# Turned queries first, weighted values last, and pooling kept to two steps of four, in a fused attention and feed-forward kernel

## The chip, the cores and the metric

The kernel runs on one core of one Trainium2 chip. The metric is device time in microseconds (us); less is better. Five engines work side by side, each through its own queue in order: TensorE (PE, matrix products), VectorE (DVE), ScalarE (ACT), GpSimd (POOL), and SyncE (SP), which here issues every DMA.

## What is computed

Attention over pooled keys and values, and a feed-forward layer with squared ReLU on its result, all in float32:

```python
# q, k, v: (8 batches, 8 heads, 576 tokens, 64)
k_p = k.reshape(B, H, Sp, 8, D).mean(axis=3)        # Sp = 72
v_p = v.reshape(B, H, Sp, 8, D).mean(axis=3)
scores = scale * np.matmul(q, k_p.transpose(0, 1, 3, 2))
attn = np.exp(scores - max); attn = attn / (sum + 1e-09)
x = np.matmul(attn, v_p) -> (4608 tokens, 512)
h = np.maximum(x @ w_in, 0.0)                        # w_in 512 x 2048
out = h * h @ w_out                                  # w_out 2048 x 512
```

The weights come in as float64 and are turned into float32 on the chip.

## The kernel before

The 4608 tokens are cut into 12 chunks (`c`) of 384. The 2048 hidden columns are cut into 16 pieces (`fc`) of 128. A *step* is one pair (c, fc); there are 192, and the loop at line 653 runs over them. In step s PE makes the hidden piece of that step (`hidden`, tile `h`, 12 products) and, two steps late (`LAG`), the product with `w_out` (`project`, tile `o`, 9 products; the first chunk has fewer). From the second chunk on, each factor is split into a high and a low part (`xh`, `xl`; `gh`, `gl`; weights `w_i`, `w_o` in two halves), so that three cheap products replace a costly one. In between, ACT and DVE take the hidden piece through ReLU (ACT, tile `r`), square (DVE, `r`), cast (ACT, `gh`) and difference (DVE, `gl`).

The attention of the chunks to come is worked in among these steps. Each chunk has four head pairs (`p`), and a pair goes through eight stages (line 637), whose steps `STEADY` sets for chunks 2 to 11 (line 80; chunk 1 has `EARLY`, chunk 0 stands ahead of the loop): `transpose_q` at step 16c - 22 + 4p, then `scores`, `exponents`, `send_sums`, `fetch_sums`, `reciprocals`, `fetch_reciprocals` and `weigh_values` 1, 3, 4, 5, 6, 7 and 8 steps later. So the steps repeat in fours. Counted by the step number modulo 4:

- 2: `transpose_q` of one pair (PE `qps`; ACT casts its high part into `st`, DVE writes the difference into `st`) and `weigh_values` of another (PE `av`; DVE multiplies into `rb`, ACT casts `xh`, DVE writes `xl`). I call this the turn step.
- 3: `scores` (PE `sps`, which reads all of `st`; ACT copies to `sc`; POOL reduces the maximum over partitions, `mx`).
- 0: `reciprocals` (DVE `rr`, from the DMA `rc`).
- 1: `exponents` (DVE and ACT on `sc`; POOL sums over partitions, `tot`).

Keys and values of a batch must be pooled before its first chunk. `kv_steps` (line 625) sets this with `KV0`, the step of its start, and `KV_AT`, four lists of offsets: key loads and reductions (`load_k`, `pool_k`, DVE `kp`), the turns of the two halves of the keys (`transpose_k`, PE `kps`), and value loads; a value is reduced (`pool_v`, DVE `vp`) two steps after its load. All loads of `q`, `k` and `v` share four buffers (`LD`, tag `ld`), and a load waits in SP's queue until its buffer is free. Six batches go this way; the first two are pooled ahead of the steps.

The order within a step is written out in the loop: `hidden`; the PE work of the step's other items, in the order of the list `later`; `project`; the split of the hidden piece of the step before; then what each item of `later` returned (its ACT and DVE work), in the same order; then the items without PE work, pooling among them; the conversion and the splitting of weights; the loads; and last the ReLU. Every engine keeps this order. Three PSUM buffers (`ps_a`) serve `qps`, `kps`, `av` and `sps` in turn.

Of the kernel before, what the change touches and what calls it, by code (L numbers as in the profile page):

```python
# [32 lines left out]
def pooled_attn_relu2_ffn(  # L33
# [44 lines left out]


    STEADY = ((-22, -18, -14, -10), (0, 1, 3, 4, 5, 6, 7, 8))  # L80
    KV0 = -31
    EARLY = ((-19, -16, -13, -10), (0, 2, 3, 5, 5, 6, 7, 8))

    KV_AT = ((0, 1, 2, 3, 4, 5), (2, 3, 4, 5, 6, 7), (5, 8), (6, 7, 8, 9, 10, 11, 12, 13))
    NKT = H * SP_ // QT
    WC = 256

# [18 lines left out]
    def issue_loads():  # L106
        for dst, src in loads:
            dma(dst, src)
        loads.clear()
# [37 lines left out]
    def to_float32(*keys):  # L147
        parts = []
        for key in keys:
            words, m = raw.pop(key).rearrange("p a (n w) -> p a n w", w=2), wf[key].rearrange("p (a n) -> p a n", a=2)  # L150
            parts.append((words, m, m.bitcast(U32)))
        for _, m, _ in parts:
            DVE.tensor_scalar(m, m, EXP_MIN, EXP_MAX, op0=ALU.max, op1=ALU.min)
        for _, _, m in parts:
            DVE.tensor_scalar(m, m, 3, 0x3FFFFFF8, op0=ALU.logical_shift_left, op1=ALU.bitwise_and)
        for words, _, m in parts:
            DVE.scalar_tensor_tensor(m, words[..., 1], 0xC0000000, m, op0=ALU.bitwise_and, op1=ALU.bitwise_or)
        for words, _, m in parts:
            DVE.scalar_tensor_tensor(m, words[..., 0], 29, m, op0=ALU.logical_shift_right, op1=ALU.bitwise_or)
# [320 lines left out]
    def hidden(c, fc):  # L480
        hp = ps_h.tile([P, 512], F32, name=f"h_{c}_{fc}", tag="h")
        cb, o = fc * P // WC, fc * P % WC
        prods = []
        for cc in range(NCC):
            key, cols = ("i", cb, cc // 2 * 2), slice(cc % 2 * WC + o, cc % 2 * WC + o + P)
            if c == 0:
                prods += [(wf[key][:, cols], xts[c][:, cc, :])]
            else:
                prods += [(wt[key][:, w, cols], xts[c][x][:, cc, :]) for w, x in ((0, 0), (0, 1), (1, 0))]
        for i, (w, x) in enumerate(prods):  # L490
            PE.matmul(hp[:, :CH], lhsT=w, rhs=x, start=i == 0, stop=i == len(prods) - 1)

        def activate():
            if c == 0:
                r = sb.tile([P, CH], F32, name=f"r_{c}_{fc}", tag="gh", bufs=LAG + 1)
            else:
                r = sb.tile([P, CH], F32, name=f"r_{c}_{fc}", tag="r", bufs=2)
            ACT.activation(r, hp[:, :CH], AF.Relu)
            if c < 2:
                ACT.activation(r, r, AF.Square)  # L500
            else:
                DVE.tensor_tensor(r, r, r, op=ALU.mult)
            gts[c, fc] = r

        return activate

    def split_hidden(c, fc):
        if c == 0:
            return
        gh = sb.tile([P, CH], F32R, name=f"gh_{c}_{fc}", tag="gh", bufs=LAG + 1)  # L510
        gl = sb.tile([P, CH], F32R, name=f"gl_{c}_{fc}", tag="gl", bufs=LAG + 1)
        split(gh, gl, gts[c, fc])
        gts[c, fc] = (gh, gl)
# [3 lines left out]
    def project(c, fc):  # L517
        if fc == 0:
            accs[c] = [ps_o.tile([P, 512], F32, name=f"o_{c}_{t}", tag=f"o{t}") for t in range(NTT)]
        g, key = gts.pop((c, fc)), ("o", fc)  # L520
        for t in range(NTT):
            tt = slice(t * P, (t + 1) * P)
            if c == 0:
                prods = [(g[:, tt], wf[key])]
            else:
                prods = [(g[x][:, tt], wt[key][:, w, :]) for x, w in ((0, 0), (0, 1), (1, 0))]
            for i, (a, w) in enumerate(prods):
                PE.matmul(accs[c][t], lhsT=a, rhs=w, start=fc == 0 and i == 0, stop=fc == NFC - 1 and i == len(prods) - 1)

        def store():  # L530
            for t in range(NTT):
                ob = sb.tile([P, DM], F32, name=f"ob_{c}_{t}", tag="ob", bufs=OB)
                ACT.copy(ob, accs[c][t])
                dma(out[c * CH + t * P:c * CH + (t + 1) * P, :], ob)

        return store if fc == NFC - 1 else None
# [88 lines left out]
    def kv_steps(b, s):  # L625
        k_at, pool_at, turn_at, v_at = KV_AT
        for i in range(NKT):
            at(s + k_at[i], load_k, b, i)
            at(s + pool_at[i], pool_k, b, i)
        for hf in range(2):  # L630
            at(s + turn_at[hf], transpose_k, b, hf)
        for h in range(H):
            at(s + v_at[h], load_v, b, h)
            at(s + v_at[h] + 2, pool_v, b, h)
# [3 lines left out]
    for c in range(1, NCH):  # L638
        first, offsets = EARLY if c == 1 else STEADY
        for b, _, _ in segments(c):  # L640
            if b not in ready:
                ready.add(b)
                kv_steps(b, c * NFC + KV0)
        for p in range(NPAIR):
# [7 lines left out]
    on_pe = (transpose_q, transpose_k, scores, token_scores, token_turn, weigh_values)  # L652
    for s in range(-PRO, len(steps) + LAG):
        todo = work.get(s, [])
        activate = hidden(*steps[s]) if 0 <= s < len(steps) else None
        later = [f(*a) for f, a in todo if f in on_pe]
        store = project(*steps[s - LAG]) if s >= LAG else None
        if 0 <= s - 1 < len(steps):
            split_hidden(*steps[s - 1])
        for f in later:  # L660
            f()
        for f, a in todo:
            if f not in on_pe + last:
                f(*a)
        keys = [a[0] for f, a in todo if f is to_float32]
        if keys:
            to_float32(*keys)
        for f, a in todo:
            if f is split_weights:
                f(*a)  # L670
        issue_loads()
        for f in (activate, store):
            if f:
                f()
# [30 lines left out]
```

## Time and profile before

| | us |
|---|---|
| median of the runs (985.11, 985.27, and one of 3297.35) | 985.27 |
| profiled execution | 978.9 |
| its span, from the first to the last instruction | 977.2 |
| PE busy | 947.3 (97%) |
| DVE busy | 629.2 (64%) |
| ACT busy | 425.8 (44%) |
| POOL busy | 401.2 (41%) |

Instructions of all helpers have one line in the trace (L29), so they are told apart by the tiles that they write and read: `st<-qps,st` is DVE's difference for turned queries, `sps<-st,kl` a product of the scores. A busy PE is not PE at its peak, since its matrix products overlap; how fast it goes is read from the starts of equal pieces of work. The granted clock is the share of TensorE's full 2.4 GHz.

### The profile page before, as it was taken

How to read it: one execution, taken by the hardware profiler on the slowest of the kernel's cores; microseconds unless marked ns; L12 is line 12 of the kernel's file. 1: busy time of each engine (PE TensorE's matmuls, PEld its weight loads, DVE VectorE, ACT ScalarE, POOL GpSimd, SP SyncE). 2: the span in 40 equal slices, each digit the busy share in tenths (PEclk: the TensorE clock that was granted, in tenths of full speed). 3: DMA queues.
4: the chain of work that ended last, by engine and by line, in shares of the span. 5: the costliest groups of instructions: out<-in, count | busy, mean ns of one | idle time of the engine just before them, and what ended most of it. 6: DMA issues, size and time to landing. Idle time of an engine off the chain costs nothing.

```text
span 977.2 us, 13363 instructions
## 1 busy us (share of the span) xinstructions
PE 947.3 (97%) x4888; PEld 785.9 (80%) x4888; DVE 629.2 (64%) x1034; ACT 425.8 (44%) x847; POOL 401.2 (41%) x209
## 2 busy tenths in 40 slices
PE   6889989999999999999999999999999999999998
PEld 5544458878888888888888888888888888888997
DVE  5869997886775555776776554777677455453221
ACT  2745457674334344334434434433443434432322
POOL 4398635463444434343435335343534434340000
PEclk9999999999999999999999999999999999999999
DMA  9944203112211002112112001211221100100000
GB/s 244 354 147 163 82 17 98 49 51 82 60 56 49 25 26 74 57 52 87 49 50 74 19 23 60 66 48 36 98 57 43 58 26 17 58 10 9 33 1 32
DMA packets 53361, 64.45 MB, mean 66 GB/s; under 512 B 14936, under 2 KB 34480, under 8 KB 53296
## 3 DMA queue, kind: packets, MB, share of 16 engines
q1 hardware_dynamic: 53296, 63.61, 20.9%
q8 instruction: 38, 0.62, 0.3%
q14 instruction: 27, 0.22, 0.1%
HBM read 53.87 MB, written 9.71 MB: 65 GB/s over the span
## 4 chain that ended last, share of the span: by engine, by line
PE 77%; DVE 13%; issue 5%; ACT 4%; POOL 0%; DMA 0%; POOLq 0%; DVEq 0%; ACTq 0%; SPq 0%
PE o L29 34%; PE h L29 33%; PE sps L29 3%; PE av L29 3%; DVE wf_o L29 3%; DVE wf_i L29 2%; PE qps L29 2%; DVE st L29 2%; DVE r L29 1%; ACT st L29 1%; DVE vp L29 1%; DVE sc L29 1%; ACT gh L29 1%; DVE rb L29 1%; ACT xh L29 1%
## 5 line engine op out<-in xcount | busy, mean ns | idle before, releaser
L29 PE MATMUL h<-xh,w_i 128*128 128x384 f32 x1408 | 389.0, 337 | 0.0
L29 PE MATMUL o<-w_o,gh 128*128 128x512 f32 x1056 | 333.7, 397 | 0.0
L29 POOL PARTITION_ALL_REDUCE tot<-sc x88 | 250.2, 2890 | 192.5 <-issue 179.3
L29 PEld LDWEIGHTS h<-xh,w_i 128*128 128x128 f32 x1408 | 258.7, 188 | 8.4 <-issue 0.5
L29 POOL PARTITION_ALL_REDUCE mx<-sc x88 | 138.2, 1618 | 268.8 <-ACT sc L29 268.8
L29 PE MATMUL h<-xl,w_i 128*128 128x384 f32 x704 | 237.9, 338 | 0.0
L29 PEld LDWEIGHTS o<-w_o,gh 128*128 128x128 f32 x1056 | 193.4, 189 | 32.8 <-issue 1.2
L29 DVE TENSOR_TENSOR gl<-r,gh 128x384 fp32r<-128x384 f32 x176 | 142.6, 810 | 107.8 <-ACT gh L29 107.0
L29 PE MATMUL o<-w_o,gl 128*128 128x512 f32 x528 | 209.0, 396 | 0.0
L29 DVE TENSOR_TENSOR r<-r 128x384 f32<-128x384 f32 x160 | 101.7, 635 | 113.7 <-ACT r L29 113.2
L29 ACT CAST gh<-r 128x384 fp32r<-128x384 f32 x176 | 90.4, 514 | 179.8 <-DVE r L29 179.3
L29 ACT ACTIVATE r<-h 128x384 f32<-128x384 f32 x192 | 94.0, 490 | 106.3 <-PE h L29 105.5
L29 PEld LDWEIGHTS h<-xl,w_i 128*128 128x128 f32 x704 | 132.1, 188 | 8.2 <-issue 0.7
L29 PEld LDWEIGHTS o<-w_o,gl 128*128 128x128 f32 x528 | 99.1, 188 | 22.2
L29 ACT CAST xh<-rb 128x384 fp32r<-128x384 f32 x44 | 22.6, 513 | 136.6 <-DVE rb L29 136.6
L29 DVE TENSOR_TENSOR st<-qps,st 64x384 fp32r<-64x384 f32 x80 | 60.6, 757 | 32.6 <-ACT st L29 32.1
L29 ACT ACTIVATE sc<-sc 72x384 f32<-72x384 f32 x88 | 43.7, 525 | 74.1 <-DVE sc L29 74.1
L29 ACT CAST st<-qps 64x384 fp32r<-64x384 f32 x80 | 59.0, 738 | 0.5
L29 DVE TENSOR_REDUCE vp<-v 72x64 f32<-72x512 f32 x48 | 51.0, 1064 | 0.4
L29 DVE TENSOR_REDUCE kp<-k 96x64 f32<-96x512 f32 x42 | 44.1, 1049 | 3.7 <-DMA k<-in_k_dram 3.7
L29 DVE TENSOR_TENSOR sc<-sc,mx 72x384 f32<-72x384 f32 x88 | 44.5, 545 | 0.0
L29 DVE TENSOR_TENSOR rb<-av,rb 128x384 f32<-128x384 f32 x44 | 24.4, 555 | 30.1 <-PE av L29 29.9
(82 smaller groups left out, 725.9 us busy)
## 6 DMA issues: line engine op xcount, KB each, us to landing
k<-in_k_dram SPq DMA_DIRECT2D x48, 192.0 KB
out_dram<-ob SPq DMA_DIRECT2D x36, 256.0 KB
rb<-rd SPq DMA_DIRECT2D x88, 96.0 KB
raw_i<-in_moe_w_in_dram SPq DMA_DIRECT2D x16, 512.0 KB
raw_o<-in_moe_w_out_dram SPq DMA_DIRECT2D x16, 512.0 KB
v<-in_v_dram SPq DMA_DIRECT2D x48, 144.0 KB
q<-in_q_dram SPq DMA_DIRECT2D x30, 192.0 KB
q<-in_q_dram SPq DMA_DIRECT2D x32, 96.0 KB
```

The costliest lines, as they stand in the source:

```text
L29: return lambda *a, **k: self.tc.keep_in_program_order(f(*a, **k))
```

## The change

Three numbers or tables and one line differ.

```diff
-    KV0 = -31
+    KV0 = -35
-    KV_AT = ((0, 1, 2, 3, 4, 5), (2, 3, 4, 5, 6, 7), (5, 8), (6, 7, 8, 9, 10, 11, 12, 13))
+    KV_AT = ((0, 1, 4, 5, 8, 9), (2, 3, 6, 7, 10, 11), (7, 12), (12, 13, 16, 17, 20, 21, 24, 25))
...
-        later = [f(*a) for f, a in todo if f in on_pe]
+        later = [f(*a) for f, a in sorted(((f, a) for f, a in todo if f in on_pe), key=lambda x: x[0] is weigh_values)]
```

`KV0` and all offsets of pooling now make its steps 3 or 0 modulo 4; the turns of keys fall into steps 0 and 1. A batch takes 28 steps from its first load to its last reduction, where it took 16; the first keys are loaded four steps earlier. The sort puts `weigh_values` behind all else in the list `later`, on PE and, since the list is also the order of what follows, on ACT and DVE.

On PE, in the turn step at chunk 4, piece 10 (`h_10`, then `av` of chunk 5 and `qps` of chunk 6), the kernel before has:

```order
 L29 MATMUL h_10_3917<-xh_2838,w_i_2_1574 128x384
 L29 MATMUL av_2_3930<-sc_2_3619,vp_2276 64x384 x2
 L29 MATMUL qps_0_3933<-ident,q_0_3776 128x96 x4
 L29 MATMUL o_0_3553<-w_o_1519,gh_8_3894 128x512 x2
 L29 MATMUL o_0_3553<-w_o_1519,gl_8_3895 128x512
```

and the changed kernel:

```order
 L29 MATMUL h_10_3912<-xh_2833,w_i_2_1573 128x384
 L29 MATMUL qps_0_3925<-ident,q_0_3776 128x96 x4
 L29 MATMUL av_2_3930<-sc_2_3628,vp_2185 64x384 x2
 L29 MATMUL o_0_3562<-w_o_1519,gh_8_3890 128x512 x2
 L29 MATMUL o_0_3562<-w_o_1519,gl_8_3891 128x512
```

`qps` and `av` have changed places; nothing else has.

On DVE, from the exponents of step 73 to the scores' step 75 (`r_9` to `gl_10`), the kernel before has:

```order
 L29 TENSOR_TENSOR sc_3_3814<-sc_3_3814,mx_3_1_3816 72x384
 L29 TENSOR_REDUCE vp_3741<-v_0_3825 72x64
 L29 TENSOR_TENSOR r_9_3914<-r_9_3914 128x384
 L29 TENSOR_TENSOR gl_9_3948<-r_9_3914,gh_9_3947 128x384
 L29 TENSOR_TENSOR rb_2_3900<-av_2_3930,rb_2_3900 128x384
 L29 TENSOR_TENSOR xl_3544<-rb_2_3900,xh_3543 128x384
 L29 TENSOR_TENSOR st_0_3954<-qps_0_3933,st_0_3954 64x2x2x96 x2
 L29 TENSOR_REDUCE vp_3741<-v_1_3863 72x64
 L29 TENSOR_TENSOR r_10_3967<-r_10_3967 128x384
 L29 TENSOR_TENSOR gl_10_3999<-r_10_3967,gh_10_3998 128x384
 L29 TENSOR_REDUCE vp_3741<-v_2_3912 72x64
```

and the changed kernel:

```order
 L29 TENSOR_TENSOR sc_3_3814<-sc_3_3814,mx_3_1_3815 72x384
 L29 TENSOR_TENSOR r_9_3909<-r_9_3909 128x384
 L29 TENSOR_TENSOR gl_9_3943<-r_9_3909,gh_9_3942 128x384
 L29 TENSOR_TENSOR st_0_3946<-qps_0_3925,st_0_3946 64x2x2x96 x2
 L29 TENSOR_TENSOR rb_2_3896<-av_2_3930,rb_2_3896 128x384
 L29 TENSOR_TENSOR xl_3558<-rb_2_3896,xh_3557 128x384
 L29 TENSOR_TENSOR r_10_3961<-r_10_3961 128x384
 L29 TENSOR_TENSOR gl_10_3993<-r_10_3961,gh_10_3992 128x384
 L29 TENSOR_REDUCE vp_3657<-v_0_3907 72x64
```

`st` stands ahead of `rb` and `xl`, and the two reductions before and behind them (`vp`) are gone; the first value of this batch is reduced behind `gl_10`.

Where two batches follow each other at once, their pooling overlaps now. DVE at chunk 2, pieces 2 to 4 (steps 35 and 36), before:

```order
 L29 TENSOR_TENSOR gl_2_2151<-r_2_2119,gh_2_2150 128x384
 L29 TENSOR_REDUCE kp_0_2163<-k_0_2051 96x64
 L29 COPY kp_0_2163<-kp_0_2163 96x64
 L29 TENSOR_TENSOR r_3_2168<-r_3_2168 128x384
 L29 TENSOR_TENSOR gl_3_2194<-r_3_2168,gh_3_2193 128x384
 L29 TENSOR_SCALAR rr_1_2197<-rc_1_2161 96x8
 L29 RECIPROCAL rr_1_2197<-rr_1_2197 96x8
 L29 TENSOR_REDUCE kp_0_2163<-k_1_2116 96x64
 L29 COPY kp_0_2163<-kp_0_2163 96x64
```

and now:

```order
 L29 TENSOR_TENSOR gl_2_2152<-r_2_2120,gh_2_2151 128x384
 L29 TENSOR_REDUCE vp_1384<-v_4_2037 72x64
 L29 TENSOR_REDUCE kp_0_1968<-k_2_2049 96x64
 L29 COPY kp_0_1968<-kp_0_1968 96x64
 L29 TENSOR_TENSOR r_3_2167<-r_3_2167 128x384
 L29 TENSOR_TENSOR gl_3_2200<-r_3_2167,gh_3_2199 128x384
 L29 TENSOR_TENSOR kl_2184<-kps_0_2186,kh_2183 128x288
 L29 TENSOR_REDUCE vp_1384<-v_5_2111 72x64
 L29 TENSOR_SCALAR rr_1_2206<-rc_1_2163 96x8
 L29 RECIPROCAL rr_1_2206<-rr_1_2206 96x8
 L29 TENSOR_REDUCE kp_3_2211<-k_3_2116 96x64
 L29 COPY kp_3_2211<-kp_3_2211 96x64
```

Each of these two steps has a value of one batch and a key of the next; before, each had a key alone, and the steps after them had one each too.

## Rows read from the trace of the kernel before

**Rows 1.** Stretch, length, busy us of PE, PEld, DVE, ACT, POOL; clock, DMA share, GB/s

```profile
30.00:150.00 120.00, 109.55 (x426) 58.51 (x424) 104.46 (x188) 64.77 (x129) 76.09 (x24) 0.99 0.43 140
...
210.00:540.00 330.00, 327.63 (x1727) 283.08 (x1726) 219.39 (x345) 141.66 (x285) 139.26 (x70) 1.00 0.18 56
```

**Rows 2.** Waits, whole span: engine, tile, awaited: total us, times, longest

```profile
DVE rr L29 <- DMA rc<-rs: 7.6, 1, 7.6
...
PE sps L29 <- DVE st L29: 8.5, 9, 2.3
```

**Rows 3.** Timeline of PE around `av`: start us, us, engine, line, what

```profile
152.04 0.87 PE L29 MATMUL av<-sc,vp 72*64 72x384 f32 x4
...
324.59 0.87 PE L29 MATMUL av<-sc,vp 72*64 72x192 f32 x8
...
343.13 0.34 PE L29 MATMUL h<-xh,w_i 128*128 128x384 f32 x1
343.39 0.87 PE L29 MATMUL av<-sc,vp 72*64 72x192 f32 x8
...
877.24 0.87 PE L29 MATMUL av<-sc,vp 72*64 72x384 f32 x4
```

**Rows 4.** Timeline of PE around one turn of keys

```profile
263.17 0.34 PE L29 MATMUL h<-xh,w_i 128*128 128x384 f32 x1
263.34 0.41 PE L29 MATMUL kps<-ident,kp 96*128 96x96 f32 x3
263.54 0.71 PE L29 MATMUL o<-w_o,gh 128*128 128x512 f32 x2
```

**Rows 5.** Timeline of all engines around one wait, steps 74 and 75; brackets: idle before

```profile
419.82 1.92 DVE L29 TENSOR_TENSOR gl<-r,gh 128x384 fp32r<-128x384 f32 x1 [0.58 <-ACT gh L29]
420.00 0.55 PE L29 MATMUL qps<-ident,q 96*128 96x96 f32 x4
...
422.24 0.51 ACT L29 CAST xh<-rb 128x384 fp32r<-128x384 f32 x1 [2.45 <-DVE rb L29]
422.66 1.70 ACT L29 CAST st<-qps 64x384 fp32r<-64x384 f32 x2
...
424.39 1.67 DVE L29 TENSOR_TENSOR st<-qps,st 64x384 fp32r<-64x384 f32 x2 [1.04 <-ACT st L29]
...
426.21 0.37 PE L29 MATMUL sps<-st,kl 128*72 128x384 f32 x1 [1.45 <-DVE st L29]
```

**Rows 6.** Timeline of DVE and PE at steps 14 and 15

```profile
130.99 0.54 DVE L29 TENSOR_TENSOR rb<-av,rb 128x384 f32<-128x384 f32 x1
...
133.71 1.70 DVE L29 TENSOR_TENSOR st<-qps,st 64x384 fp32r<-64x384 f32 x2 [1.04 <-ACT st L29]
...
135.55 0.46 PE L29 MATMUL sps<-st,kl 128*72 128x384 f32 x1 [2.29 <-DVE st L29]
...
137.70 1.92 DVE L29 TENSOR_TENSOR w_i<-wf_i,w_i 128x512 fp32r<-128x512 f32 x2
```

**Rows 7.** Timeline of DVE and POOL in the round after rows 5

```profile
426.10 1.06 DVE L29 TENSOR_REDUCE vp<-v 72x64 f32<-72x512 f32 x1
...
428.63 2.87 POOL L29 PARTITION_ALL_REDUCE mx<-sc  x2 [6.46 <-ACT sc L29]
...
429.67 0.55 DVE L29 TENSOR_TENSOR r<-r 128x384 f32<-128x384 f32 x1
...
443.81 1.68 DVE L29 TENSOR_TENSOR st<-qps,st 64x384 fp32r<-64x384 f32 x2 [1.04 <-ACT st L29]
```

**Rows 8.** Instructions of tiles `r` and `kp`: ns least/median/most, first and last start

```profile
L29 DVE TENSOR_TENSOR gl<-r,gh x176: 541/559/1991, 145.7 to 968.9; 128x384 fp32r<-128x384 f32 x176
...
L29 DVE TENSOR_REDUCE kp<-k x42: 998/1052/1094, 3.5 to 718.9; 96x64 f32<-96x512 f32 x42
L29 DVE COPY kp<-kp x42: 190/193/933, 4.5 to 719.9; 96x64 f32<-96x64 f32 x42
```

**Rows 9.** PE by stretch: busy, granted clock, DMA share, GB/s

```profile
136.00:138.00 2.00, 2.00 (x6) 0.50 0.03 8
```

## The prediction

> **What bounds the kernel now.** I read busy times by stretch first: in the long middle, 210 to 540 us, TensorE (PE) is busy 327.63 of 330 us, VectorE (DVE) 219.39 [rows 1]. So only two things count there: what PE executes, and where it stands still. The waits say where: of all that PE waits for, one line repeats, the scores `sps` waiting for DVE's `st`, 8.5 us in 9 waits, the longest 2.3 [rows 2].
>
> How much is there in all? The program repeats every four steps (one head pair), and each round has one `av`. From the `av` at 152.04 to that at 877.24 lie 38 rounds, 725.2 us [rows 3]. A quiet round, 324.59 to 343.39, takes 18.80 [rows 3]; 38 of them would be 714.4. The transposes of new keys (`kps`) take 0.20 each (263.34 to 263.54) [rows 4]; the 12 of them take 2.4. Left over: 725.2 - 714.4 - 2.4 = 8.4 us. That is about the most that a better order can free in the long middle part. As idle time of PE, the trace shows 8.5 - 2.3 = 6.2 us of it, in eight waits. The ninth is the one at 135.55 [rows 6].
>
> One wait in full [rows 5]: in the turn step, `qps` is issued on PE at 420.00, after `av`. ScalarE (ACT) has the cast `xh` in its queue ahead of the two `st` casts; `xh` stands 2.45 us until DVE's `rb`, and DVE gets to `rb` only after a `gl` of 1.92 us. So ACT casts `st` from 422.66, DVE subtracts from 424.39, and PE's `sps`, ready 1.45 us before, starts at 426.21.
>
> **The change, part by part.**
>
> *Turned queries first (the sorted list).* Nothing is added or removed: `qps` moves ahead of `av` on PE, and ACT's and DVE's work for it ahead of `xh`, `rb`, `xl`. In rows 5 `qps` would start at about 419.2, end within 0.5, and ACT (its `gh` done at 419.8; the next thing in its queue is `xh`) could cast `st` from 419.8 to 421.5; DVE, busy with `gl` until 421.74, subtracts from 421.74 to 423.4 (1.67 as in the row). `sps` was wanted at 426.21 - 1.45 = 424.76 and starts without a wait, 1.3 us to spare. What is late instead: `rb`, `xh`, `xl` move from 421.7 - 423.4 to about 423.4 - 425.1. Queued behind them are ACT's relu of the same step and DVE's `r`. `xl` of the last pair is read two steps after, some 9 us on; the relu frees the PSUM buffer for `h` two steps on. Cost: nothing, covered by those two steps.
>
> *Order of PE alone.* Going from `h` into `av` takes 0.26 (343.13 to 343.39) where `h` into `kps` takes 0.17 (263.17 to 263.34) [rows 3, 4]. If `qps` ahead of `av` saves that 0.09 in each of about 40 turn steps, it is 3.6 us; if `av` pays it behind `qps`, nothing. I take 0, since the row belongs to `av`, which still loads new weights; 3.6 goes into the range.
>
> *Pooling only in steps 3 and 0 of four.* The same 84 reductions (36 of keys, 48 of values) of the same durations, 1.06 for a value's (426.10, [rows 7]) and 1.05 for a key's, with a copy of 0.19 in the median and 0.93 at most behind it [rows 8]. They leave the turn step and the exponents' step, where they stood ahead of `st`. In exchange the six batches now need 28 steps each, not 16, so the second of each pair of neighbours pools its keys while the first pools its values. In these stretches each pooling step has one of each, 1.06 + 1.05 + about 0.25 for the copy = 2.4 us, two such steps a round. Does DVE still make its round? In rows 5 and 7, from the end of `st` at 426.06 to its end at 445.49, DVE needed 19.43 us with four value reductions in it (the one at 426.10 is the first; 4.24 together). Now it loses the 1.04 in which `st` waited for ACT [rows 7], and has 4.8 of pooling in place of 4.24: 19.43 - 1.04 + 0.56 = 18.95, against PE's 18.80, or 19.00 with a `kps`. DVE loses some 0.1 us a round for three rounds, against 1.3 to spare. I put 0.5 us for the whole as what may remain.
>
> *The middle part in sum:* between the visible 6.2 and the 8.4 I take 7.3, less 0.5: **-6.8 us**.
>
> *The wait at 135.55.* Here DVE is the busy one, with the weights. It comes to `rb` at 130.99 and is done with `st` at 135.41 (133.71 + 1.70); `sps` waits 2.29 [rows 6]. In the new order ACT casts `st` while DVE is still at its weights, and DVE can subtract where `rb` now stands, from 130.99 to 132.7, before PE asks (135.55 - 2.29 = 133.26). But the next `h`, the first of chunk 1, needs the weight difference that DVE makes from 137.70 to 139.62 [rows 6], and this moves only by what DVE no longer stands idle, the 1.04 before `st`. The new keys' pooling at steps 15 and 16 comes behind it. The gain lies between 0.5 (PE then waits at that `h`) and 3.5 (2.29 and the price of the clock below); I take **-2.0 us**.
>
> After that wait the granted clock is 0.50, its lower level of 1.2 GHz, from 136 to 138 [rows 9]; those 2 us at half rate hold 1 us of work, and with the edges I put their price at 1.2. The Trainium skill (TensorE: Matmul & The Clock Gate, "Part 1: The HAM clock gate") says that the low rate is the default and that steady work releases it; the row agrees in that the low rate comes behind the wait. By that rule the half-rate piece goes if PE works through, and the gain here would be nearer 3; if PE merely waits a little later, it stays, and the gain is nearer 1.
>
> *The SP queue.* Loads share four buffers. A load whose buffer isn't free holds the queue, and what is issued behind it. Today a round with pooling makes five loads too (four of a batch and one `q`), and DVE's `rr`, the reader of `rc`, waited for its DMA only once in the whole trace, 7.6 us [rows 2], which is the longest that a hold has cost. In the doubled stretches the fifth load of a round is held until a reduction one step later, with `rc` behind it; `rr` is due a step later still. I take 0; 7.6 is the other end.
>
> **Sum.** -6.8 - 2.0 = -8.8. The profiled execution took 978.9 us (span 977.2), so it becomes 970.1. The median of the runs shown is 985.27, 6.4 above the profiled one; I carry the difference over: 985.27 - 8.8 = **976.5 us**.
>
> **Rivals.**
>
> 1. *The waits stay.* If `sps` is held by something else that the releaser row hides, or if the freed time returns as PE waiting at `kps` (the last keys of a half are still reduced only one step before they are turned), less than half comes. For it: `kps` follows a doubled pooling step by one `h`. Against it: the quiet rounds show PE at its own pace with `st` as the only late thing. Gain 0 to 4: **981 to 985**.
>
> 2. *DVE becomes the bound in the doubled stretches: slower.* `gl` takes 0.56 in the median but up to 1.99 [rows 8]; the long one in rows 5 lies under GpSimd's sum all-reduce `tot`. The change shifts `r` and `gl` of the turn step later, toward the maximum all-reduce `mx`. If that held both by 1.4 each, a DVE round would be 2.8 longer: three rounds lose 3 x 2.9 - 1.3 = 7.4 us, three stretches 22: 985.27 - 8.8 + 22 = **998**. It decides from a growth g with 3 x (3g - 1.3) > 8.8, so 1.4 us a round. Against it: the `r` at 429.67 takes 0.55 in the middle of an `mx` that runs from 428.63 to 431.50 [rows 7]. The Trainium skill (SBUF — State Buffer, "SBUF: two separate sides") has this as an exclusive lock that a GpSimd operation and a VectorE operation with two SBUF inputs take from each other for a whole instruction. By that rule the hold would come under `mx` too; the row at 429.67 does not show it.
>
> 3. *The early part speeds up as well.* From 30 to 150 us PE is busy 109.55 of 120 [rows 1]; the scores now go ahead of `av` at steps 5, 8 and 11. But DVE is busy 104.46 there, and its work is the same. If all 10 us went: **966**.
>
> **How the numbers follow.** Forecast (gain of 4 to 14): 0.72. Rival 1: 0.16. Rival 2: 0.05. Rival 3: 0.05. A loss by the SP queue, up to 7.6: 0.02. The forecast's own range is 971 (8.4 + 3.5 + 3.6 with nothing left, less a little) to 981; with rival 1 and part of rival 3 the range is 968 to 985. About 2% is what a measurement of this kernel can tell from no change; that is 965.6 or 1005. Faster 0.02, same 0.95, slower 0.03.
>
> **What would show it.** PE waiting for DVE `st` falls from 8.5 us to under 1.5. Rounds stand at 18.7 to 19.1 throughout, those of the doubled stretches too; a round over 19.5 there speaks for rival 2, a new PE wait at `kps` for rival 1. `xh` no longer ends before `st`. The clock at 136 to 138 is 1.00 if the first wait is gone. I am wrong if PE's idle time in the middle is as large as before under another name, or if the quiet rounds change by more than 0.1 us, since then the order of `qps` and `av` has a price of its own.

## The result, and the profile after

The changed kernel takes 973.37 us (median of 971.6 to 975.2), the kernel before 985.19 beside it: a ratio of 0.988, 95% interval 0.985 to 0.991. It is faster by 1.2%, which is within 2%. The forecast was 976.5, range 968 to 985.

The profiled execution took 971.68 us, 969.9 of it the span. I cut it where PE starts the first `h` of a step, since step 16 is the first of chunk 1, with the split products, in both kernels. In the kernel before (PE's timeline, start us, us, engine, line, what; steps 0, 16 and 191):

```profile
40.62 2.85 PE L29 MATMUL h<-x,wf_i 128*128 128x384 f32 x8
...
140.10 0.73 PE L29 MATMUL h<-xh,w_i 128*128 128x384 f32 x1
...
964.83 0.33 PE L29 MATMUL h<-xh,w_i 128*128 128x384 f32 x1
```

and in the changed kernel:

```profile
43.83 0.91 PE L29 MATMUL h<-x,wf_i 128*128 128x384 f32 x2
...
140.02 0.73 PE L29 MATMUL h<-xh,w_i 128*128 128x384 f32 x1
...
957.62 0.33 PE L29 MATMUL h<-xh,w_i 128*128 128x384 f32 x1
```

| us | before | after | difference |
|---|---|---|---|
| up to step 0 | 40.62 | 43.83 | +3.21 |
| steps 0 to 16, the early part | 99.48 | 96.19 | -3.29 |
| steps 16 to 191, the middle | 824.73 | 817.60 | -7.13 |
| behind it | 12.33 | 12.31 | -0.02 |

The first row has nothing to do with the change, as the last section shows. Between these two executions the rest is worth 3.29 + 7.13 = 10.4 us, but 1.6 us of the early part is not the order's. Behind the wait at step 15 the execution of the kernel before runs at a granted clock of 0.50 [rows 9], TensorE's lower level of 1.2 GHz. A kernel that comes below (old pooling, turns in step 0) has the same instructions up to step 24. It waits as long at that place, and runs on at the full 2.4 GHz (timeline of PE; then length, busy us of PE, PEld, DVE, ACT, POOL; clock, DMA share, GB/s):

```profile
141.44 0.37 PE L29 MATMUL sps<-st,kl 128*72 128x384 f32 x1 [2.30 <-DVE st L29]
```

```profile
142.00:144.00 2.00, 2.00 (x7) 1.04 (x6) 1.93 (x4) 1.97 (x5) 0.68 (x1) 1.00 0.04 8
```

Its early part takes 97.84 us; a stretch at half rate at its step 5 is made good by steps 7 to 10. Four more kernels with the wait of 2.3 us take 97.8 to 97.9, and a fifth 98.5, by 0.7 us more at step 7. Against 97.84 the change gains 1.65 us in the early part, and 8.8 us in all.

The stretches that answer to [rows 1] and [rows 9] (length, busy us of PE, PEld, DVE, ACT, POOL; clock, DMA share, GB/s):

```profile
30.00:150.00 120.00, 111.28 (x453) 60.46 (x452) 105.80 (x197) 63.73 (x124) 72.92 (x22) 1.00 0.43 142
210.00:540.00 330.00, 330.00 (x1747) 288.77 (x1746) 222.82 (x348) 144.50 (x289) 140.49 (x72) 1.00 0.19 57
136.00:138.00 2.00, 2.00 (x10) 1.32 (x9) 1.66 (x4) 2.00 (x5) 0.00 (x0) 1.00 0.23 70
```

and the waits that answer to [rows 2]:

```profile
PE sps L29 <- DVE st L29: 1.0, 2, 0.7
...
PE kps L29 <- DVE kp L29: 0.4, 1, 0.4
```

PE is busy all of the 330 us, the wait for `st` has gone from 8.5 us in nine to 1.0 in two, and the clock from 136 to 138 is 1.00. Steps 74 and 75, which [rows 5] show before, look like this (timeline of all engines; brackets: idle before):

```profile
415.93 5.01 POOL L29 PARTITION_ALL_REDUCE tot<-sc  x2 [6.79 <-issue]
...
417.89 0.49 PE L29 MATMUL qps<-ident,q 96*128 96x96 f32 x4
...
418.46 1.70 ACT L29 CAST st<-qps 64x384 fp32r<-64x384 f32 x2
418.59 1.92 DVE L29 TENSOR_TENSOR gl<-r,gh 128x384 fp32r<-128x384 f32 x1 [0.58 <-ACT gh L29]
420.52 1.69 DVE L29 TENSOR_TENSOR st<-qps,st 64x384 fp32r<-64x384 f32 x2
422.24 0.56 DVE L29 TENSOR_TENSOR rb<-av,rb 128x384 f32<-128x384 f32 x1
422.83 0.51 ACT L29 CAST xh<-rb 128x384 fp32r<-128x384 f32 x1 [2.67 <-DVE rb L29]
...
423.38 0.34 PE L29 MATMUL sps<-st,kl 128*72 128x384 f32 x1
```

`gl` is as long as before and lies as late. But ACT casts `st` while it runs, DVE subtracts right behind it, and `st` is done at 422.21, 1.17 us before PE asks for it. `rb`, `xh` and `xl` now come behind `st`, and nobody waits for them.

### The profile page after: what moved, and what is told of

It is laid out like the page before. It is cut to its first block, busy times and chain, and to the rows that moved or that the text cites. A ratio compares the mean times of both kernels' runs of the same rounds, so it can differ in the third digit from the quotient of the medians.

```text
span 969.9 us, 13344 instructions
## 1 busy us (share of the span) xinstructions
PE 946.1 (98%) x4888; PEld 793.5 (82%) x4888; DVE 628.5 (65%) x1034; ACT 428.3 (44%) x847; POOL 394.1 (41%) x209
## 4 chain that ended last, share of the span: by engine, by line
PE 85%; DVE 8%; issue 3%; DMA 2%; ACT 1%; POOL 0%; SPq 0%; DVEq 0%; POOLq 0%
PE o L29 38%; PE h L29 37%; PE av L29 4%; PE sps L29 3%; DVE wf_o L29 2%; DVE wf_i L29 2%; PE qps L29 1%; PE vps L29 1%; DMA q<-in_q_dram 1%; DMA rd<-rr 0%; DVE st L29 0%; PE kps L29 0%; DVE sc L29 0%; DVE kp L29 0%; POOL tot L29 0%
## 5 line engine op out<-in xcount | busy, mean ns | idle before, releaser
L29 POOL PARTITION_ALL_REDUCE mx<-sc x88 | 131.4, 1540 | 243.6 <-ACT sc L29 243.6
L29 DVE TENSOR_TENSOR gl<-r,gh 128x384 fp32r<-128x384 f32 x176 | 146.5, 832 | 108.4 <-ACT gh L29 106.5
L29 DVE TENSOR_TENSOR r<-r 128x384 f32<-128x384 f32 x160 | 105.7, 661 | 108.7 <-ACT r L29 108.3
L29 PE MATMUL av<-sc,vp 72*64 72x384 f32 (+1 forms) x256 | 43.1, 425 | 0.9 <-ACT sc L29 0.9
```

Of the source, the lines that this page charges most:

```text
L29: return lambda *a, **k: self.tc.keep_in_program_order(f(*a, **k))
```

## The experiments

All kernels by the same cuts. The time is that of the profiled execution; the last column is PE's `sps` waiting for DVE's `st` in the whole span, and how often.

| kernel | time | step 0 starts | early part | middle | wait, times |
|---|---|---|---|---|---|
| before | 978.9 | 40.6 | 99.5 | 824.7 | 8.5, 9 |
| the change | 971.7 | 43.8 | 96.2 | 817.6 | 1.0, 2 |
| sort alone | 973.1 | 47.0 | 96.2 | 815.9 | 0.7, 1 |
| new pooling alone | 989.8 | 41.0 | 97.9 | 836.9 | 16.7, 16 |
| sort on PE alone, new pooling | 998.9 | 46.8 | 97.9 | 840.2 | 20.3, 31 |
| sort on ACT and DVE alone, new pooling | 968.8 | 40.5 | 96.3 | 818.0 | 0.4, 1 |
| new pooling, ACT casts `st` first | 993.4 | 46.6 | 97.8 | 835.0 | 14.8, 27 |
| new pooling, one sum of two | 978.6 | 43.6 | 96.5 | 824.4 | 3.4, 3 |
| new pooling, copies for reductions | 982.3 | 44.2 | 97.8 | 826.3 | 8.9, 8 |
| new pooling, turns in step 0 | 984.7 | 42.6 | 97.9 | 830.1 | 11.5, 10 |
| new pooling, copies and turns in step 0 | 974.1 | 41.2 | 98.5 | 820.4 | 3.8, 2 |
| old pooling, turns in step 0 | 981.8 | 46.5 | 97.8 | 823.4 | 7.4, 7 |
| old pooling, turns in step 0, sort | 966.6 | 40.5 | 96.2 | 815.9 | 0.7, 1 |
| old pooling, sort from step 12 on | 968.6 | 40.9 | 96.7 | 817.0 | none |

Compare the two columns early part and middle; the time also holds the start, which varies by 6 us. Two middles hold a stretch at half rate too, behind the wait at step 19: those of the new pooling alone and of the one with one sum. In the new pooling alone (columns as above):

```profile
160.00:162.00 2.00, 2.00 (x7) 1.63 (x6) 2.00 (x4) 1.82 (x5) 0.99 (x1) 0.50 0.02 4
```

Step 19 takes 8.64 us there. In the kernel with new pooling and turns in step 0, whose instructions are the same up to step 24, it waits as long, runs on at 1.00 and takes 7.16. So I estimate 835.4 for the middle of the new pooling alone at the full rate (836.9 - 1.5); no other kernel of the table has such a stretch in its middle.

### Each part alone

The sort without the pooling table:

```diff
-        later = [f(*a) for f, a in todo if f in on_pe]
+        later = [f(*a) for f, a in sorted(((f, a) for f, a in todo if f in on_pe), key=lambda x: x[0] is weigh_values)]
```

> The kernel before with the sorted list alone; pooling stays where it was (every step of a batch's 16, the turn step among them). Theory A: each of the two parts alone is enough for the waits in the middle. With the sort, ACT casts st before it stands for rb, and that is worth 1.3 us where the pooling costs 1.06 at most; so PE's wait for DVE st falls from 8.5 to under 2.0 us, the middle (first product of chunk 1 to the last step: 824.7 before, 817.6 with the whole change) is 817 to 819, and the time lies within 2 us of the changed kernel's 973.4. Rival B: the two parts add up, the reductions ahead of st still make it late; wait 3 to 5, middle 820 to 823, time 976 to 980.

Measured: 971.28 us median, ratio to before 0.988 [0.984, 0.991]. The pooling table without the sort:

```diff
-    KV0 = -31
+    KV0 = -35
-    KV_AT = ((0, 1, 2, 3, 4, 5), (2, 3, 4, 5, 6, 7), (5, 8), (6, 7, 8, 9, 10, 11, 12, 13))
+    KV_AT = ((0, 1, 4, 5, 8, 9), (2, 3, 6, 7, 10, 11), (7, 12), (12, 13, 16, 17, 20, 21, 24, 25))
```

> The changed kernel with the sort undone: pooling in steps 3 and 0 alone, av and its ACT and DVE work ahead of qps again. Theory A: the eight waits of the middle are gone (they all lay in rounds with pooling), but the wait at step 15 stays (2.3 us and the half clock), since no pooling made that one, and st stays late by about 0.1 in quiet rounds: early part (step 0 to 16) 99 to 101, middle 818 to 820, time 977 to 980. Rival B: half of the middle's gain is left, middle 820 to 823, time 980 to 983. Rival C: in the doubled stretches, where st now has less to spare, waits come in anew: PE's wait for DVE st over 6, time 983 or more.

Measured: 991.12 us median, ratio 1.009 [1.006, 1.011]. The sort alone gives all of the gain, and its middle is 1.7 us shorter than that of the whole change. The new pooling alone is slower than before, beyond the rival C of its expectation: 12.2 us more in the middle, 10.7 without the stretch at half rate, with the wait for `st` doubled. So the two parts don't add up: the second is harmful alone, and the sort hides that harm.

### The sort on PE alone, and on ACT and DVE alone

Both with the new pooling. First only PE's order is sorted, and what follows stays in the old order:

```diff
-        later = [f(*a) for f, a in sorted(...)]
+        made = {}
+        for f, a in sorted(((f, a) for f, a in todo if f in on_pe), key=lambda x: x[0] is weigh_values):
+            made[f, a] = f(*a)
+        later = [made[f, a] for f, a in todo if f in on_pe]
```

> The changed kernel, but sorted on PE alone: qps ahead of av on PE, while ACT and DVE do the work on av first, as before. It asks whether the order on PE or the order behind it frees the time. Theory A: the order on ACT and DVE does it (xh, standing for rb, ahead of st); then the trace is near that of the sort undone: middle 818 to 820, the wait at step 15 back (early part 98.5 to 100). Rival: it is enough that qps is 0.8 us earlier; early part near 96.2 and middle 817.6 as in the whole change.

Then the reverse:

```diff
-        later = [f(*a) for f, a in sorted(...)]
+        made = [(f, f(*a)) for f, a in todo if f in on_pe]
+        later = [g for _, g in sorted(made, key=lambda x: x[0] is weigh_values)]
```

> The changed kernel, but with av ahead of qps on PE as before, while ACT and DVE do st first and rb, xh, xl last. Theory A: nearly all of the whole change: early part 96 to 97, middle 817.5 to 818.5. Rival (PE order matters): middle over 819 or early part over 98. In either case a turn step shows what the order on PE costs by itself: 5.49 us in quiet rounds before, 5.51 after the change, so I expect 5.49 here, and no price.

The middle is 840.2 with PE's order alone and 818.0 with that of ACT and DVE alone, where the whole sort has 817.6. The gain lies in the two queues behind PE. With `qps` ahead of `av` on PE alone it gets worse (31 waits), quiet score steps among them (5.32 us each at steps 59, 63 and 67, with the new pooling alone 5.00). `av` then ends later, and `rb`, `xh` and the old `st` hang on it: in the quiet step 58 `rb` starts 3.44 us into the step, with the new pooling alone 3.11. A quiet turn step takes 5.49 us with PE's old order, as expected, and 5.51 with the new one.

### Why the new pooling alone is slow

My first thought was that DVE has too much to do where two batches overlap. Its busy time in such a stretch says no, 14.96 of 20 us (columns as above):

```profile
480.00:500.00 20.00, 18.68 (x97) 15.87 (x96) 14.96 (x23) 7.64 (x15) 7.86 (x4) 1.00 0.19 55
```

The timeline shows a chain instead. New pooling alone, from the exponents of one step to the scores two steps on:

```profile
481.40 1.02 DVE L29 TENSOR_TENSOR sc<-sc,mx 72x384 f32<-72x384 f32 x2
481.98 1.00 ACT L29 ACTIVATE sc<-sc 72x384 f32<-72x384 f32 x2 [1.09 <-DVE sc L29]
482.66 5.01 POOL L29 PARTITION_ALL_REDUCE tot<-sc  x2 [7.17 <-issue]
482.88 0.47 ACT L29 ACTIVATE r<-h 128x384 f32<-128x384 f32 x1
483.39 1.35 DVE L29 TENSOR_TENSOR r<-r 128x384 f32<-128x384 f32 x1 [0.97 <-ACT r L29]
...
485.32 1.92 DVE L29 TENSOR_TENSOR gl<-r,gh 128x384 fp32r<-128x384 f32 x1 [0.58 <-ACT gh L29]
...
487.16 0.55 DVE L29 TENSOR_TENSOR rb<-av,rb 128x384 f32<-128x384 f32 x1
487.74 0.51 ACT L29 CAST xh<-rb 128x384 fp32r<-128x384 f32 x1 [2.45 <-DVE rb L29]
488.16 1.68 ACT L29 CAST st<-qps 64x384 fp32r<-64x384 f32 x2
...
489.87 1.67 DVE L29 TENSOR_TENSOR st<-qps,st 64x384 fp32r<-64x384 f32 x2 [1.02 <-ACT st L29]
...
491.69 0.36 PE L29 MATMUL sps<-st,kl 128*72 128x384 f32 x1 [1.31 <-DVE st L29]
```

DVE's subtraction `sc` starts the exponents, these start GpSimd's two sums `tot`, and while the sums run DVE's `r` takes 1.35 in place of 0.55 and `gl` 1.92 in place of 0.56. `gl` ends at 487.24, 0.43 before the second sum does (487.67). Behind `gl` wait `rb`, then ACT's `xh`, ACT's `st`, DVE's `st`, PE's `sps`. Whatever makes `sc` late makes `st` late. In quiet rounds `sc` starts 0.31 us into its step. At steps 37 and 85 it starts 2.95 us in with the new pooling alone and 0.50 before, and the waits two steps on, at 39 and 87, are new. At steps 41, 73 and 89 it starts 3.35 us in in both kernels, and the waits two steps on are the same. In the changed kernel it is as late (2.94 and 3.35), and nobody waits. Each link of this chain can be taken out.

*The hold by the second sum.* From chunk 2 on, the second of the two sums is left out:

```diff
-            GP.partition_all_reduce(tots[i], sc[:, i], channels=SP_, reduce_op=bass_isa.ReduceOp.add)
-        live[c, p] = (sc, tots)
+            if i == 0 or c < 2:
+                GP.partition_all_reduce(tots[i], sc[:, i], channels=SP_, reduce_op=bass_isa.ReduceOp.add)
+        live[c, p] = (sc, tots if c < 2 else [tots[0], tots[0]])
```

> The new pooling steps with the old order, but from chunk 2 on GpSimd sums only the first head of a pair over the partitions, and that sum stands for both heads (the second sum is left out, so the second head's normalisation is not computed). GpSimd's tot takes 2.5 us in place of 5.0. Theory D: gl of the turn step is held until 0.4 us before the end of the second sum (1.92 us in place of 0.56); without the second sum it takes 0.56, rb, xh and st come 1.36 us earlier, the waits of 1.3 to 1.45 us nearly vanish, PE waiting for DVE st falls from 16.7 to about 5 us (weight phase left), steps 16 to 191 to about 824 us. If the hold has no part in it: 835 to 838 us.

The same round:

```profile
477.70 2.51 POOL L29 PARTITION_ALL_REDUCE tot<-sc  x1 [7.17 <-DVE sc L29]
...
480.36 0.56 DVE L29 TENSOR_TENSOR gl<-r,gh 128x384 fp32r<-128x384 f32 x1 [0.58 <-ACT gh L29]
...
483.55 1.71 DVE L29 TENSOR_TENSOR st<-qps,st 64x384 fp32r<-64x384 f32 x2 [1.03 <-ACT st L29]
...
485.40 0.36 PE L29 MATMUL sps<-st,kl 128*72 128x384 f32 x1
```

From `gl`'s start to `st`'s start: 3.19 us, before 4.55, and no wait is left. Of all 176 `gl` (ns least/median/most, first and last start; new pooling alone, then with one sum):

```profile
L29 DVE TENSOR_TENSOR gl<-r,gh x176: 546/559/1919, 148.4 to 979.7; 128x384 fp32r<-128x384 f32 x176
```

```profile
L29 DVE TENSOR_TENSOR gl<-r,gh x176: 548/559/986, 149.7 to 968.6; 128x384 fp32r<-128x384 f32 x176
```

The wait fell from 16.7 to 3.4 us and the middle by 12.5, to 824.4, as expected (824); both middles hold the stretch at half rate. The hold by GpSimd's second sum is a link.

*ACT's place for `st`.* ACT casts `st` ahead of everything else in its step; DVE keeps `rb`, `xl`, `st` (in short; the casts are taken out of what `transpose_q` returns):

```diff
+        for f in later:
+            if hasattr(f, "cast"):     # the two ACT.copy of transpose_q
+                f.cast()
         for f in later:
             f()
```

> The new pooling steps with the old order (no sort), but ScalarE casts the turned queries into st ahead of everything else of its step; VectorE keeps the old order rb, xl, st, and TensorE too. Theory D (chain): in the run with the new pooling alone, st was late at the end of a chain: exponents' sc, GpSimd's tot, which holds VectorE's r and gl, then rb, ScalarE's xh, its two st casts, VectorE's st. ScalarE's casts were done 1.04 us after xl; without that stand each wait of 1.3 to 1.45 us falls to about 0.3, PE waiting for DVE st from 16.7 us to 6 (mostly in the weight phase before 210 us), and steps 16 to 191 from 836.9 to about 825 us. Rival E (VectorE has too much to do in the rounds with double pooling): the order on ScalarE frees nothing, 834 to 838 us.

That missed: 835.0 in place of 825, which is 0.4 less than the 835.4 of the new pooling alone at the full rate. The long waits did shrink, to at most 0.49 from step 31 on, but some twenty score steps now have one of that size, quiet ones among them. In the same round:

```profile
489.17 1.71 ACT L29 CAST st<-qps 64x384 fp32r<-64x384 f32 x2 [0.91 <-PE qps L29]
490.14 0.54 DVE L29 TENSOR_TENSOR rb<-av,rb 128x384 f32<-128x384 f32 x1
490.90 0.51 ACT L29 CAST xh<-rb 128x384 fp32r<-128x384 f32 x1
...
491.45 0.56 DVE L29 TENSOR_TENSOR xl<-rb,xh 128x384 fp32r<-128x384 f32 x1 [0.77 <-ACT xh L29]
492.02 1.67 DVE L29 TENSOR_TENSOR st<-qps,st 64x384 fp32r<-64x384 f32 x2
...
493.84 0.36 PE L29 MATMUL sps<-st,kl 128*72 128x384 f32 x1 [0.49 <-DVE st L29]
```

Now `xh` stands behind ACT's `st`, and DVE's `st` still stands behind `xl`, which needs `xh`. The wait moved from one queue to the other. The two queues must be sorted together. (DVE's alone can't be: its `st` would stand for ACT's `st`, this behind `xh`, `xh` for `rb`, and `rb` behind DVE's `st`.)

*What makes `sc` late: the reductions.* From batch 2 on, copies of one row of eight stand in place of the reductions of keys and values, so the pooling is left out (in short):

```diff
-        DVE.tensor_reduce(kv[b][2][:, h, :], ...)
+        DVE.tensor_copy(kv[b][2][:, h, :], vt[:, :D])     # and the same for kp
```

> The new pooling steps with the old order, but from batch 2 on each reduction of keys and values is a copy of one of its eight rows (pooling over the eight is left out): about 0.2 us in place of 1.05. Theory D: sc and tot are then on time in every round, and steps 16 to 191 take about 818 us, as with the sort, with PE waiting for DVE st under 3 us in them. Rival F (it is the turns of keys or the queue of loads at their new steps that cost, not the reductions): 830 us or more.

Half right: the middle fell by 10.6 us, 9.1 of them not the half rate, but to 826.3 and not 818. The waits at steps 39, 71, 83, 87 and the like are gone; those at steps 27, 43, 75, 91, 123 and 139 stand as they were. All six come two steps after the turn of the second half of a batch's keys. In the round of step 75:

```profile
418.62 0.41 PE L29 MATMUL kps<-ident,kp 96*128 96x96 f32 x3
...
419.51 0.46 DVE L29 TENSOR_TENSOR kl<-kps,kh 128x288 fp32r<-128x288 f32 x1 [2.58 <-ACT kh L29]
419.88 1.01 DVE L29 TENSOR_TENSOR sc<-sc,mx 72x384 f32<-72x384 f32 x2
```

DVE stands idle for 2.58 us until `kl` can start, with `sc` queued behind it. So `sc` is held by a wait and not by work, and the turns, rival F of that run, have a share. But not by a new step: 8 from a start of -31 and 12 from -35 are the same step, and the kernel before has these six waits at the same length.

*What makes `sc` late: the turns.* One number moves the second turn out of the exponents' step, into a step 0; here with the new pooling, then with the copies as well:

```diff
-    KV_AT = (..., (7, 12), ...)
+    KV_AT = (..., (7, 15), ...)
```

> The new pooling steps with the old order, the second half of the keys turned at offset 15 in place of 12, again a step 0 in place of an exponents' step. Theory G: of the 12.2 us that the new pooling steps cost in the old order, and of the 7 before, only the waits after those turns go: steps 16 to 191 fall from 836.9 to about 830.5 us, and the waits after the steps with double pooling (steps 39, 71, 83, 87, 119, 131, 135) stay.

> As the run with copies in place of reductions (pooling over the eight rows is left out from batch 2 on), new pooling steps, old order, and the second half of the keys turned at offset 15. Both suspected causes of a late tot are gone. Theory G: the waits for st that were left there (1.45 us at steps 75 and 123, 0.2 at 43, 91, 139, 1.65 at 27) vanish, and steps 16 to 191 fall from 826.3 to about 820 us. If something else makes tot late, more than 824 us.

830.1 and 820.4, as expected (830.5 and 820). Taken from 835.4, the middle at the full rate, the second turn costs 5.3 us, the reductions 9.1, and both together 15.0. The kernel before has the second turn too, at the same steps. So the loss of 10.7 us against it lies mainly with the reductions' new steps; the first turn, which moved from the turn step to step 0, was not tested apart. Without the two, the old order comes within 3 us of the sorted one.

### The same turn in the kernel before

If the turn in the exponents' step is a cause, moving it should mend the kernel before without any sort:

```diff
-    KV_AT = (..., (5, 8), ...)
+    KV_AT = (..., (5, 11), ...)
```

> The kernel before, with one number changed: the second half of a batch's keys is turned three steps later (offset 11 in place of 8), which moves it from the exponents' step (1 modulo 4) to a step 0. Theory G: six of the kernel before's waits for st (at steps 27, 43, 75, 91, 123, 139) come two steps after such a turn, because VectorE's kl of that turn stands ahead of the exponents' subtraction sc, which makes GpSimd's tot late, and with it gl, rb, xh and st. Then PE waiting for DVE st falls from 8.5 us to about 2.5 (the wait at step 15 stays), and steps 16 to 191 from 824.7 to about 818 us, without any sort; the time falls by 6 us or so, ratio about 0.993. If the turns have no part in it, steps 16 to 191 stay at 824 or more.

Mostly missed: the ratio is 0.998 [0.995, 1.000], the middle 823.4 and not 818. The waits at steps 43, 91 and 139 are gone and those at 75 and 123 fell from 1.45 to 0.33, but the ones a round later (79, 127) rose from 0.5 to 1.10, 27 kept 1.41, and step 19 has a new one of 0.83. The moved turn now stands one step ahead of the exponents of step 77, whose `sc` starts 2.72 us into it, before 2.00. With the old pooling a reduction stands in every step, also beside the exponents. Which of these keeps `sc` late there wasn't separated. With the sort on top:

> The same with the sort. Theory G: the sort takes st off the end of that chain, so where the turns stand no longer matters: steps 16 to 191 take 815.9 us within 0.5, as with the sort alone, and steps 0 to 16 96.2. Rival: the two add up, 812 us or less.

The middle is 815.87, to the hundredth that of the sort alone: once `st` is off the chain, where the turns stand doesn't matter. Its lower median (968.3 us, ratio 0.986 [0.982, 0.990]) is not a better kernel: early part and middle equal those of the sort alone, and its profiled execution merely reached step 0 at 40.5 us, not 47.0.

### The early part

With the change, steps 15 and 14 fell from 9.58 and 6.95 us to 5.45 and 6.49 (1.6 of this is the half rate), but steps 11 and 12 rose from 6.81 and 6.18 to 7.72 and 6.58: at step 11 the scores stand ahead of `av`, and now wait 0.68 for `st`. So I sorted from step 12 on only, with the old pooling:

```diff
-key=lambda x: x[0] is weigh_values
+key=lambda x: s >= 12 and x[0] is weigh_values
```

> The old pooling with the sort only from step 12 on, so that in steps 5, 8 and 11 (chunk 1's scores and weighted values in one step) the old order stays. With the sort alone, steps 11 and 12 took 0.9 and 0.4 us longer than before, since the scores now wait for DVE's st at step 11. Theory: those 1.3 us come back, steps 0 to 16 take about 94.9 us (96.2 with the sort throughout, 99.5 before), steps 16 to 191 stay at 815.9. Rival: the later start of step 12 was covered by the weights' conversion, and steps 0 to 16 stay at 96.2.

The rival held: the early part is 96.7, not 94.9; without 0.66 us that step 7 took longer, ahead of any sort, it is 96.0. What steps 11 and 12 won back, steps 14 to 16 lost again (6.97, 6.08 and 4.84 us, with the change 6.49, 5.45 and 4.67). PE waits there for two results of DVE's work on the weights, 0.22 and 0.19 us; the rest of the loss wasn't traced.

## Why the prediction was right, and where it was not

- **The middle, -6.8 within 6.2 to 8.4: -7.13.** Right in mechanism and size. From step 28 to 175 the score steps give 7.82 us (37 of them took 187.33, now 179.51), step 27 another 1.86, the turn steps 0.51; steps 0 of four, where the first turn of keys now stands, give back 1.56, and steps 18 to 26 1.40. That more is freed than the visible waits was right too: `sps` starts late also where the trace shows no wait. Before, `st` ends at 348.75 and `sps` starts at 348.89, 0.25 behind the last product of `h` and not 0.17; the score steps of such rounds took 5.00 us and now 4.88. By this quiet rounds changed by up to 0.12 us (18.85, now 18.73), a little over the 0.1 that was named as a sign of being wrong. The order of `qps` and `av` is not the reason: the turn step took 5.49 and takes 5.51.
- **The mechanism in rows 5.** Right: `st` follows `gl` at once, `sps` has 1.17 us to spare (1.3 said), `xh` and `rb` wait and hold nobody.
- **PE's order alone, 0.** Right: 818.0 with PE's old order, 817.6 with the new.
- **The wait at 135.55, -2.0 within 0.5 to 3.5: -3.29, of which the order gives 1.65.** DVE does subtract before it goes on, and `sps` doesn't wait:

```profile
131.09 0.87 PE L29 MATMUL av<-sc,vp 72*64 72x192 f32 x8
131.20 1.71 ACT L29 CAST st<-qps 64x384 fp32r<-64x384 f32 x2 [1.28 <-PE qps L29]
133.40 1.71 DVE L29 TENSOR_TENSOR st<-qps,st 64x384 fp32r<-64x384 f32 x2
135.13 0.56 DVE L29 TENSOR_TENSOR rb<-av,rb 128x384 f32<-128x384 f32 x1
```

 The half-rate piece behind the wait is gone, the clock from 136 to 138 is 1.00: PE worked on and kept the high rate. That agrees with the case that the Trainium skill's rule (TensorE: Matmul & The Clock Gate, "Part 1: The HAM clock gate") spoke for. But it can't be counted as a gain of the order: six other kernels have the same wait of 2.3 us at step 15 and keep the high rate behind it. The prediction's price of the clock came from the one execution that was profiled. Steps 14 and 15 gained 4.6 us, 3.0 of them without the half rate; 1.3 went back at steps 11 and 12, where I had looked for no loss. The order's own 1.65 is near the -2.0, and within the range.
- **Pooling only in steps 3 and 0, a loss of 0.5: 1.7 with the sort, 10.7 without.** This is the step that failed, although the sum hides it. I counted reductions per round and found DVE's round of 18.95 us against PE's 18.80. But what counts is not DVE's round; it is what stands ahead of the exponents' `sc` and so sets when GpSimd's sums hold `gl`. I had read the `gl` of 1.92 us in rows 5 as a given, and the "1.04 in which `st` waited" as the whole story; both were the end of a chain that begins two steps earlier. In the old order this move costs 10.7 us (12.2 with the half rate). With the sort it costs 1.7, mostly at steps 18 to 26 (45.58 us, with the sort alone 43.97), where key reductions that now begin at step 15 lie among the weights; the one wait of PE at `kps`, 0.4 us, is there too.
- **The SP queue, 0.** Right: `rr` waits for `rc` once, 7.6 us, as in [rows 2].
- **The sum and the carry.** -8.8 said; -10.4 between the two profiled executions, -8.8 without the half rate. That this is the forecast's sum to the tenth is luck: the sort alone gives 8.9 in the middle where 7.3 was put, and the pooling takes 1.7 of it where 0.5 was put. The medians lie 11.8 apart. I had carried over 6.4 us between the profiled execution and the median, and that belongs to a few executions: the kernel before took 984.6 to 985.3 us in the three behind its median, and 978.1 to 984.8 in thirteen later ones, with a median of 982.03. Against that one the changed kernel is 8.7 us faster. So some 3 us of the measured 11.8, and with it the 3.1 by which the time is below the forecast, look like the draw of executions. Those three have no trace, so where they lost time is not shown.
- **Rivals.** The waits did not stay (1). Rival 2 has its place right, the doubled stretches, and its link right, a GpSimd reduction that holds DVE, but it sought it under `mx`, where the hold is short (last section), and took DVE's busy time for the bound. Without the sort the doubled stretches do become slower, by that link. The early part did speed up (3), by 1.65 of the 10 us that were left there.

## What to carry to other kernels

Where an in-order queue has a wait, follow what stands ahead of the waiting instruction two or three steps back, across engines, before putting a price on moving anything: a busy share of 75% says nothing when the queue's front waits. Take the result that another engine needs next off the end of the chain, in all queues that it passes through at once; sorting one of two queues moved the wait and little else. Measure the parts of a change apart: here one number table was harmful and the other line hid it. And look at the granted clock of each execution before taking one from another: a stretch at half rate of 1.5 us comes and goes with the same instructions.

## What the runs showed of the hardware

GpSimd's sum over partitions holds a DVE operation with two SBUF inputs until about 0.4 us before its end: `gl` of 1.92 us ends at 487.24, the sum at 487.67, and without that sum no `gl` is over 0.99. In the kernel before, 12 `r` and 30 `gl` of over 1.2 us all end 0.43 us before the sum does. The Trainium skill (SBUF — State Buffer, "SBUF: two separate sides") has this as an exclusive lock for a whole instruction; the rows agree but for the last 0.4 us, and spans of GpSimd are rough in this profile. Under `mx` the hold is shorter. In the changed kernel (timeline of all engines):

```profile
312.73 1.50 POOL L29 PARTITION_ALL_REDUCE mx<-sc  x1
...
313.25 0.80 DVE L29 TENSOR_TENSOR gl<-r,gh 128x384 fp32r<-128x384 f32 x1 [0.58 <-PE o L29]
```

This `gl` takes 0.80 in place of 0.56 and ends 0.18 before `mx` does. The `r` of 0.55 [rows 7], which the prediction read as a sign against a hold, starts 1.04 us into a pair of `mx` of 2.87 together, about 0.4 before the first of the two ends, so that row can't speak against a hold.

Behind one and the same wait of PE the clock can fall or not: after 2.29 us it was 0.50 from 136 to 138 us in the kernel before [rows 9], after 2.30 us 1.00 from 142 to 144 in the kernel with turns in step 0. Between the first step and the last, PE stands for 2.0 to 2.3 us 26 times in the fourteen kernels, at steps 5, 12, 15 and 19. Behind six of these the clock is 0.50 for a while, behind twenty it stays at 1.00. What decides it the rows don't show.

All fourteen kernels have the same instructions before step 0, and yet they differ by 3 or 6 us there: step 0 starts at 40.5 to 41.2, 42.6 to 44.2, or 46.5 to 47.0. The same 24 products take 2.78 us in all kernels of the first group, 4.3 to 4.8 in the second and 5.3 in the third. Before, and then with the sort alone (timeline of PE):

```profile
13.82 2.78 PE L29 MATMUL vps<-vv,ones 96*72 96x128 f32 x24
```

```profile
15.08 5.32 PE L29 MATMUL vps<-vv,ones 96*72 96x128 f32 x24
```

The granted clock of the two stretches reads alike (length, busy us by engine, clock, DMA share, GB/s):

```profile
13.80:16.50 2.70, 2.70 (x27) 2.57 (x24) 1.36 (x4) 1.09 (x3) 0.24 (x1) 1.00 1.08 277
```

```profile
15.00:20.30 5.30, 5.30 (x26) 5.01 (x24) 1.19 (x4) 1.09 (x3) 3.57 (x9) 1.00 1.07 256
```

So the clock's row does not show this difference, and the work's own pace does. The Trainium skill (TensorE: Matmul & The Clock Gate, "Part 1: The HAM clock gate") says that the slow stretch at a kernel's start varies from run to run; that would fit, but that it is this, the rows don't settle. For reading: kernels that differ by 1% are compared from step 0 on, not by their time alone.
